# A layer stack on one core: a shorter load of x ahead of the key weights, two fewer dummy matmuls, and the order lists that go with it

## The chip, the cores and the metric

The kernel runs on one core of a Trainium2 chip. The metric is the device time of one execution in microseconds (us); lower is better. Three runs of the kernel before gave 327.53, 329.68 and 484.78 us, with a median of 329.68. The profiled execution took 327.5 us.

## The reference

Two layers, each applied twice with the same weights: a linear attention (32 heads of 16) and an MLP with gelu. The input of each is normalised first, and the MLP normalises it a second time inside. All inputs and the output are bf16; x is 2048 x 512.

```python
def _A_ref(x, wqkv, wo):                    # D = 512, H = 32, Dh = 16
    q, k, v = split(x @ wqkv)
    phi = lambda t: jnp.where(t > 0, t + 1, jnp.exp(t)) + 1e-6
    pq, pk = phi(q), phi(k)
    kv = jnp.einsum("bhsd,bhse->bhde", pk, v)
    z = jnp.einsum("bhsd->bhd", pk)
    num = jnp.einsum("bhqd,bhde->bhqe", pq, kv)
    den = jnp.einsum("bhqd,bhd->bhq", pq, z)[..., None] + 1e-6
    return (num / den).reshape(B, S, D) @ wo

def _B_ref(x, w1, b1, w2, b2):              # F = 1792
    h = _gelu(_layernorm(x) @ w1 + b1)
    return h @ w2 + b2

x = x + _A_ref(_layernorm(x), wqkv, wo)
x = x + _B_ref(_layernorm(x), w1, b1, w2, b2)
x = x + _A_ref(_layernorm(x), wqkv, wo)
x = x + _B_ref(_layernorm(x), w1, b1, w2, b2)
```

## The kernel before

**Tiles.** The 2048 tokens are 16 tiles of 128, in 4 chunks of 4. Tile `st` is tile `k` of chunk `c` (`st = 4c + k`). In the names of operations the first digit is the round (0 or 1), the rest the tile or chunk: `K0_5` is the key projection of tile 5 in the first round.

**What is done to a tile of x in the first round.** VectorE takes its statistics (`statsA0_`, line 773, and `aggrA0_`, line 775); VectorE or GpSimd adds epsilon (`vepsA0_`, line 780); GpSimd raises it to the power -1/2 (`powA0_`, line 782); VectorE or ScalarE normalises it (`normA0_`, lines 795 and 790). Tile 3 takes its sums on ScalarE (`sumA0_3` and `sqA0_3`, lines 764 and 768, with `negA0_3` on GpSimd between). The tile is then transposed: tiles 0 to 5 on TensorE (`PTA0_`, line 817) with a copy out of PSUM (`tcA0_`, line 827), the others by a transposing DMA that SP issues (`TA0_`, line 804). Four matmuls make the keys (`K0_`, line 866), ScalarE and VectorE apply phi (`expk0_`, `reluk0_`, `mink0_`, `phik0_`, lines 837 to 854), and four matmuls add the tile to the Gram matrix of normalised x and phi of the keys (`G0_`, line 958). `Z0_` (line 941) sums the keys over the tokens, `Q0_` (lines 883 and 896) makes the queries. The key sums and the matrix go through small operations (`zb`, `KV`, `M`, `cp`) to one 512-wide matrix, `WO` applies it, and `D` (line 1074) or a sum on VectorE makes the denominators.

**The MLP** is `W1` (line 1127), gelu on ScalarE (line 1132) and `W2` (line 1163); in the last round the result goes out through the stores `OD` that SP issues.

**Dummies.** TensorE begins with matmuls of constant ones into a PSUM bank that nothing reads (`warm0`, `warm1`, line 747). `WARM` holds their widths, one list per operation.

**Loads.** `LOADS` gives each load a name, its queue (SP or ScalarE), what it loads (x by chunk and tiles, or the halves of the key or query weights), the range, and a load or operation behind which it is issued. Tile 0 of x is `x0`, tiles 1 to 3 are `x1`, `wk0` and `wk1` are the halves of the key weights, `xc1` to `xc3` the other chunks of x, `wq` the query weights. The rest of the weights go out on GpSimd's queue once all transposes of the first round are there (`wv`, `wo`, `w1_`, `w2_`). `b2` (128 KB, one row spread to 128 partitions) and `b1` go out on SP's queue; `b1` overwrites a zeroed buffer (`b1z`, GpSimd), and `Tb1` transposes it.

**Order.** Nothing is scheduled on the chip: `ORDER` lists, for each of the five engines, every operation in the order of issue, `PLACES` lists which tile uses which buffer slot after which, and `WAY` picks an engine or a form for some operations. `Settled` reads them, `assign_waits` puts a semaphore wait in front of an operation only where an earlier wait does not imply it. An engine runs its list strictly in order, so an operation that waits holds everything behind it; SP's transposes, stores and loads are one such list.

Of the kernel before, what the change touches and what calls it, by code (L numbers as in the profile page):

```python
# [185 lines left out]
def assign_waits(graph, order, sems, dma_sems):  # L186
# [10 lines left out]
    while len(done) < total:  # L197
        moved = False
        for e in ENGINES:
# [42 lines left out]
    WARM=[[512, 512, 512, 512, 512, 512, 512, 512, 512, 512, 512], [512, 512, 512, 512]],  # L242
    LOADS=[['x0', 'sp', 'x', 0, 0, 1, ''], ['x1', 'sp', 'x', 0, 1, 4, ''], ['wk0', 'sp', 'wk', 0, 0, 2, ''], ['wk1', 'act', 'wk', 0, 2, 4, 'ones'], ['xc1', 'act', 'x', 1, 0, 4, 'x0'], ['xc3', 'act', 'x', 3, 0, 4, ''], ['wq', 'act', 'wq', 0, 0, 4, ''], ['xc2', 'act', 'x', 2, 0, 4, '']],
    ORDER={
        "sp":
            "x0 x1 wk0 TA0_7 TA0_6 TA0_8 TA0_14 TA0_15 TA0_13 TA0_12 b2 TA0_10 TA0_11 TA0_9 b1 Tb1 TB0_1 TB0_0 TB0_2 TB0_3 "
            "TP0_2_0 TP0_2_1 TB0_7 TB0_4 TB0_5 TB0_6 TP0_2_3 TP0_3_3 TP0_2_2 TP0_3_2 TA1_0 TB0_9 TB0_10 TB0_8 TP0_3_1 TP0_3_0 "
            "TB0_11 TA1_5 TB0_15 TB0_12 TB0_14 TB0_13 TA1_2 TA1_7 TA1_3 TA1_1 TA1_6 TA1_4 TA1_9 TA1_8 TA1_10 TA1_11 TA1_12 "
            "TA1_13 TA1_15 TA1_14 TP1_1_0 TP1_1_1 TP1_1_2 TB1_2 TB1_3 TP1_1_3 TP1_3_1 TB1_5 TB1_4 TB1_7 TB1_6 OD1 TP1_3_0 "
            "TP1_2_1 TP1_3_3 OD0 TP1_2_0 TP1_3_2 TP1_2_3 TP1_2_2 OD2 TB1_15 TB1_13 TB1_12 TB1_14 OD5 OD3 TB1_10 TB1_9 TB1_11 "  # L250
            "TB1_8 OD7 OD4 OD13 OD6 OD14 OD12 OD10 OD8 OD9 OD11 OD15_0 OD15_1",
        "pe":
            "warm0 warm1 PTA0_0 PTA0_1 K0_0 PTA0_2 K0_1 PTA0_3 K0_2 PTA0_4 G0_0_0 K0_3 K0_4 Q0_0_0 G0_1_0 PTA0_5 Q0_0_1 K0_5 "
            "G0_2_0 Z0_0 G0_3_0 K0_6 K0_7 K0_8 G0_4_0 Q0_1_2 K0_14 G0_5_0 K0_15 G0_6_0 G0_7_0 Q0_1_0 K0_12 Z0_1 K0_13 K0_10 "
            "K0_11 K0_9 Q0_1_3 Q0_1_1 Q0_0_3 Q0_0_2 G0_8_0 Z0_3 Z0_2 G0_9_0 G0_10_0 D0_0_0 G0_11_0 G0_12_0 D0_0_2 G0_13_0 "
            "G0_14_0 D0_0_3 D0_0_1 D0_1_1 G0_15_3 D0_1_0 G0_15_1 G0_15_2 ZR0 G0_15_0 Q0_2_0 Q0_2_1 KV0_0 KV0_1 KV0_2 KV0_3 "
            "Q0_2_2 M0_1 M0_0 M0_3 D0_1_2 M0_2 Q0_2_3 WO0_0_0 D0_1_3 WO0_0_1 WO0_0_2 WO0_0_3 WO0_1_0 WO0_3_0 WO0_2_0 Q0_3_1 "
            "Q0_3_0 WO0_4_0 WO0_7_0 WO0_5_0 Q0_3_2 Q0_3_3 WO0_6_0 W10_0_0_0 W10_0_13_0 W10_0_3_0 W10_0_2_0 W10_0_6_0 "
            "W10_0_9_0 W10_0_11_0 W10_0_5_0 W10_0_8_0 W10_0_1_0 W10_0_4_0 W10_0_12_0 W10_0_10_0 W10_0_7_0 W20_0_0 W20_1_0 "
            "W10_0_2_1 W10_0_7_1 W10_0_5_1 W10_0_11_1 W20_0_7 W20_1_7 W10_0_1_1 W10_0_9_1 W10_0_12_1 WO0_9_0 W10_0_0_1 "  # L260
            "W10_0_6_1 W10_0_8_1 W10_1_1_0 W10_1_6_0 WO0_8_0 W10_0_4_1 W10_1_7_0 W10_1_10_0 W10_1_8_0 W10_1_11_0 W10_1_3_0 "
            "W10_1_9_0 W10_0_13_1 W10_1_5_0 W10_1_4_0 W10_1_13_0 WO0_11_0 W10_1_0_0 W10_1_12_0 W10_1_2_0 W10_0_3_1 W10_0_10_1 "
            "WO0_15_0 W20_4_0 W20_5_0 W20_5_7 WO0_10_0 W20_4_7 K1_0 WO0_14_0 W20_7_0 W20_6_0 W20_7_7 W20_6_7 W20_3_0 W20_2_0 "
            "W20_2_7 WO0_13_0 W10_2_6_0 W10_2_0_0 WO0_12_0 W10_2_5_0 W20_3_7 W10_2_12_0 W10_2_9_0 W10_2_4_0 W10_2_3_0 "
            "W10_2_2_0 W10_2_1_0 W10_2_13_0 W10_2_8_0 W10_2_11_0 W10_2_10_0 W10_2_7_0 W20_10_0 W20_11_0 W20_9_0 W20_9_7 "
# [12 lines left out]
            "W21_6_0 W21_5_0 W21_4_0 W21_5_7 W21_4_7 W11_3_10_0 W11_3_0_0 W21_7_0 W11_3_7_0 W11_3_1_0 W21_6_7 W11_3_3_0 "
            "W11_3_2_0 W21_7_7 W11_3_8_0 W11_2_7_0 W11_3_11_0 W11_3_13_0 W11_3_4_0 W11_3_6_0 W11_3_12_0 W11_2_9_0 W11_3_9_0 "
            "W11_3_5_0 W11_2_3_0 W11_2_5_0 W21_14_0 W11_2_2_0 W21_13_0 W21_12_0 W11_2_6_0 W21_12_7 W21_13_7 W11_2_11_0 "  # L280
            "W11_2_0_0 W21_14_7 W11_2_4_0 W11_2_13_0 W11_2_1_0 W11_2_12_0 W11_2_8_0 W11_2_10_0 W21_8_0 W21_9_0 W21_10_0 "
            "W21_8_7 W21_10_7 W21_9_7 W21_15_h0 W21_11_0 W21_11_7 W21_15_h1",
        "act":
            "wk1 xc1 xc3 sumA0_3 wq sqA0_3 tcA0_0 xc2 tcA0_1 expk0_0 tcA0_2 reluk0_0 tcA0_3 expk0_1 reluk0_2 reluk0_1 tcA0_4 "
            "expk0_2 reluk0_3 expk0_3 normA0_7 expq0_0_0 expk0_4 tcA0_5 reluq0_0_0 normA0_8 expk0_5 reluq0_0_1 normA0_14 "
            "expq0_0_1 reluk0_5 expk0_6 normA0_15 expk0_8 normA0_13 reluk0_8 expk0_7 expk0_14 reluk0_7 normA0_10 expq0_1_2 "
            "reluk0_14 expk0_15 normA0_11 expq0_1_0 expk0_12 reluk0_13 expk0_13 expk0_10 reluk0_11 expk0_11 expk0_9 "
            "reluq0_1_3 expq0_1_3 reluq0_1_1 expq0_0_3 expq0_1_1 expq0_0_2 reluq0_0_2 ln0_0_0 rec0_0_0 ln0_0_2 rec0_0_2 "
            "ln0_0_3 ln0_0_1 rec0_0_3 cpz0 rec0_0_1 expq0_2_0 ln0_1_1 rec0_1_1 ln0_1_0 rec0_1_0 cpm0_0 cpm0_1 expq0_2_1 "
# [1040 lines left out]
```

## Time and profile before

The page of the profiled execution, 327.5 us by the clock of the runs, with a span of 326.3 us from the first to the last instruction:

| | busy us | share of the span | instructions |
|---|---|---|---|
| TensorE matmul (PE) | 322.2 | 99% | 1723 |
| TensorE weight load (PEld) | 159.3 | 49% | 1723 |
| VectorE (DVE) | 211.0 | 65% | 503 |
| ScalarE (ACT) | 193.1 | 59% | 334 |
| GpSimd (POOL) | 152.5 | 47% | 224 |

Busy time counts an engine's instructions whatever they wait for next; a matmul's own length (0.63 us at the start, 0.38 us later, for 512 columns) holds its way through the array, so the time between two starts is the better measure of what one costs. The chain of waits goes back from the last instruction, at each step to what released it. "Idle before, releaser" behind a row is how long the engine had stood and what ended that. SPq, ACTq and POOLq are the queues of these engines, with their DMA issues.

Loads move 20.4 MB in all. In the first 12 us they are 3.15 MB.

### The profile page before, as it was taken

Reading aid. Unit: us, or ns where it says so; the run is one execution under the profiler, and the core shown is the slowest. Engines: PE = TensorE matmul, PEld = TensorE weight load, DVE = VectorE, ACT = ScalarE, POOL = GpSimd, SP = SyncE. Lnnn points to the kernel's source line nnn. Section 1 sums busy time; section 2 is a strip of 40 time slices with the busy share of each in tenths; the row PEclk is TensorE's granted clock in tenths of the full one; section 3 lists DMA queues with packets and bytes.
Section 4 is the critical chain, followed back from the end, with each engine's and each line's share of the span. In section 5 each row is a group of like instructions: output and inputs, shape, how many; then the busy total and the mean of one; then the engine's idle time right before and its main releaser. Section 6 shows DMA issues by size and latency. Waiting matters only on the chain.

```text
span 326.3 us, 4763 instructions
## 1 busy us (share of the span) xinstructions
PE 322.2 (99%) x1723; PEld 159.3 (49%) x1723; DVE 211.0 (65%) x503; ACT 193.1 (59%) x334; POOL 152.5 (47%) x224
## 2 busy tenths in 40 slices
PE   8999999999999999999999999999999999999997
PEld 3444445576454444444444444458644444444444
DVE  5987679996938685142436899999989983300112
ACT  4988769797661416529673477969833454551600
POOL 5662548588663417300757434783856593100000
PEclk9999999999999999999999999999999999999999
DMA  7355753334012210331011110012034322200102
GB/s 266 120 83 97 219 189 104 105 64 68 16 32 50 54 26 3 80 64 34 0 32 33 34 32 0 19 32 50 17 82 94 69 48 66 64 0 2 64 0 80
DMA packets 46883, 20.37 MB, mean 62 GB/s; under 512 B 41932, under 2 KB 45388, under 8 KB 46860
## 3 DMA queue, kind: packets, MB, share of 16 engines
q1 hardware_dynamic: 44572, 13.00, 18.8%
q0 software_dynamic: 1056, 4.72, 4.5%
q10 hardware_dynamic: 1232, 2.36, 2.0%
q8 instruction: 13, 0.21, 0.3%
q14 instruction: 10, 0.08, 0.1%
HBM read 8.00 MB, written 2.10 MB: 31 GB/s over the span
## 4 chain that ended last, share of the span: by engine, by line
PE 97%; DVE 1%; ACT 1%; issue 0%
PE ps L1127 30%; PE ps L1163 29%; PE ps L1097 9%; PE ps L866 8%; PE ps L883 5%; PE ps L987 4%; PE ps L958 4%; PE ps L896 2%; PE ps L747 2%; PE ps L1150 1%; PE ps L1074 1%; PE ps L1008 1%; PE ps L1031 1%; PE ps L941 1%; PE ps L817 0%; DVE pkb L854 0%
## 5 line engine op out<-in xcount | busy, mean ns | idle before, releaser
L1132 ACT ACTIVATE gT<-ps,b1c 128x512 bf16<-128x512 f32 (+1 forms) x140 | 77.1, 600 | 65.3 <-PE ps L1127 65.0
L1127 PE MATMUL ps<-t,w 128*128 128x512 bf16 (+1 forms) x560 | 102.2, 336 | 0.0
L1163 PE MATMUL ps<-w,gT 128*128 128x512 bf16 x434 | 97.6, 379 | 0.0
L1127 PEld LDWEIGHTS ps<-t,w 128*128 128x128 bf16 x560 | 54.6, 98 | 43.7 <-ACT t L827 0.3
L1163 PEld LDWEIGHTS ps<-w,gT 128*128 128x128 bf16 x434 | 42.5, 98 | 50.4 <-DVE xsb L1169 0.2
L782 POOL TENSOR_TENSOR rstd<-veps,neghalf 128x1 f32<-128x1 f32 x64 | 37.9, 602 | 33.5 <-DVE veps L780 31.4
L837 ACT ACTIVATE eb<-ps 128x512 bf16<-128x512 f32 x64 | 37.4, 614 | 18.3 <-PE ps L866 10.5
L1173 DVE TENSOR_TENSOR outb<-ps,xsb 128x512 bf16<-128x512 f32 x15 | 10.1, 686 | 46.3 <-PE ps L1163 40.3
L773 DVE BATCH_NORM_STATS2 stats<-xsb 128x6 f32<-128x512 f32 x48 | 32.3, 678 | 0.4
L848 ACT ACTIVATE rb<-ps 128x512 bf16<-128x512 f32 x45 | 26.6, 617 | 9.2 <-PE ps L866 8.7
L866 PE MATMUL ps<-wqkv,t 128*128 128x512 bf16 x128 | 31.6, 379 | 0.1
L1097 PE MATMUL ps<-gtb,t 128*128 128x512 bf16 x128 | 31.2, 379 | 0.1
L850 DVE TENSOR_SCALAR eb<-eb 128x512 bf16<-128x512 bf16 x45 | 14.0, 321 | 21.1 <-ACT eb L837 21.1
L1113 POOL TENSOR_TENSOR xsb<-xsb,b2b 128x512 f32<-128x512 f32 x20 | 24.3, 1224 | 6.8 <-ACT yb L790 6.6
L790 ACT ACTIVATE yb<-xsb,nmr,rstd 128x512 bf16<-128x512 f32 x21 | 16.7, 812 | 14.2 <-POOL nmr L787 13.9
L780 POOL TENSOR_SCALAR veps<-mv 128x1 f32<-128x1 f32 x35 | 7.6, 217 | 30.8 <-DVE mv L775 28.1
L1063 POOL TENSOR_TENSOR t<-t,rr 128x512 bf16<-128x512 bf16 x14 | 15.5, 1114 | 13.6 <-DVE rr L1059 12.9
L795 DVE TENSOR_SCALAR yb<-xsb,mv,rstd 128x512 bf16<-128x512 f32 x27 | 16.1, 602 | 8.5 <-POOL rstd L782 8.3
L1051 POOL TENSOR_TENSOR lr<-t,zrow 128x512 f32<-128x512 bf16 x15 | 17.9, 1191 | 5.7 <-ACT zrow L971 4.2
L883 PE MATMUL ps<-wqkv,t 128*128 128x512 bf16 x80 | 19.9, 379 | 0.0
L1097 PEld LDWEIGHTS ps<-gtb,t 128*128 128x128 bf16 x128 | 12.3, 98 | 14.7 <-DVE rr L1059 0.6
L866 PEld LDWEIGHTS ps<-wqkv,t 128*128 128x128 bf16 x128 | 12.0, 98 | 14.9 <-ACT t L827 1.0
(97 smaller groups left out, 373.5 us busy)
## 6 DMA issues: line engine op xcount, KB each, us to landing
w<-in_B_w_dram POOLq DMA_DIRECT2D x4, 896.0 KB, 6.9
out_dram<-outb SPq DMA_DIRECT2D x15, 128.0 KB, 1.9
t<-in_A_x_dram ACTq DMA_DIRECT2D x3, 512.0 KB, 4.6
t<-yb SPq DMA_TRANSPOSE x56, 2.5
wqkv<-in_A_wqkv_dram ACTq DMA_DIRECT2D x1, 512.0 KB, 5.8
wqkv<-in_A_wqkv_dram POOLq DMA_DIRECT2D x1, 512.0 KB, 4.6
wo<-in_A_wo_dram POOLq DMA_DIRECT2D x1, 512.0 KB, 5.5
t<-in_A_x_dram SPq DMA_DIRECT2D x1, 384.0 KB, 3.1
```

The lines of the kernel that those rows point to most:

```text
L773: G.op("dve", lambda e: e.bn_stats(stats[:, s.slot, :], src()), 620, reads=src_keys, writes=[k + "s"], tiles=[s, *src_tiles], name=f"stats ...
L782: G.op("pool", lambda e: e.tensor_tensor(rstd[:, s.slot:s.slot + 1], veps[:, s.slot:s.slot + 1], neghalf[:], op=ALU.pow), 570, reads=[k + ...
L837: G.op("act", lambda e: e.activation(eb[:, et.slot, :], bank(bt), ACT.Exp), 478, reads=[src_key], writes=[f"e{tag}"], tiles=[bt, et], name ...
L848: G.op("act", lambda e: e.activation(rb[:, rt.slot, :], bank(bt), ACT.Relu), 478, reads=[src_key], writes=[f"r{tag}"], tiles=[bt, rt], nam ...
L866: ins = e.matmul(bank(b), lhsT=yTa(yT)[:, dt, k * P:(k + 1) * P], rhs=wqkv[:, dt, D:2 * D], start=(dt == 0), stop=(dt == DT - 1))
L883: ins = e.matmul(bank(b), lhsT=yTa(yT)[:, dt, k * P:(k + 1) * P], rhs=wqkv[:, dt, 0:D], start=(dt == 0), stop=(dt == DT - 1))
L1051: lambda e, r=r, tok=tok: e.tensor_tensor(lr[:, r.slot, :], tok(), zrow[:], op=ALU.mult), 1150 if on_pool else 600,
L1097: ins = e.matmul(bank(wb), lhsT=yTa(pq)[:, kt, k * P:(k + 1) * P], rhs=gtb[:, kt, :], start=(kt == 0), stop=(kt == DT - 1))
L1113: G.op("pool" if on_pool else "dve", lambda e: e.tensor_tensor(xsb[:, st, :], xsb[:, st, :], b2b[:], op=ALU.add), 1120 if on_pool else 600 ...
L1127: ins = e.matmul(bank(b, n), lhsT=w1[:, dt, ft * P:(ft + 1) * P], rhs=yTa(yT)[:, dt, k0 * P:k1 * P], start=(dt == 0), stop=(dt == DT - 1))
L1132: G.op("act", lambda e, ft=ft, b=b, k0=k0, k1=k1, n=n: e.activation(gT[:, g.slot, ft * 512 + k0 * P:ft * 512 + k1 * P], bank(b, n), ACT.Ge ...
L1163: ins = e.matmul(bank(b), lhsT=gT[:, g.slot, ft * 512 + k * P:ft * 512 + (k + 1) * P], rhs=w2[:, ft, :], start=(ft == 0), stop=(ft == FT - 1))
```

## The change

`LOADS` splits the load of tiles 1 to 3 of x: tile 1 alone stays in front (`x1`), tiles 2 and 3 (`x2`) go out on ScalarE's queue behind the second half of the key weights. `WARM` has 13 dummies instead of 15, and the first transpose on TensorE stands between the first 11 and the last 2. The five order lists, 56 of 68 lists of buffer slots and 61 entries of `WAY` are written anew with it; no operation but `x2` is added and none but the two dummies is removed.

```diff
-    WARM=[[512, 512, 512, 512, 512, 512, 512, 512, 512, 512, 512], [512, 512, 512, 512]],
-    LOADS=[['x0', 'sp', 'x', 0, 0, 1, ''], ['x1', 'sp', 'x', 0, 1, 4, ''], ['wk0', 'sp', 'wk', 0, 0, 2, ''], ['wk1', 'act', 'wk', 0, 2, 4, 'ones'], ['xc1', 'act', 'x', 1, 0, 4, 'x0'], ['xc3', 'act', 'x', 3, 0, 4, ''], ['wq', 'act', 'wq', 0, 0, 4, ''], ['xc2', 'act', 'x', 2, 0, 4, '']],
+    WARM=[[512, 512, 512, 512, 512, 512, 512, 512, 512, 512, 512], [512, 512]],
+    LOADS=[['x0', 'sp', 'x', 0, 0, 1, ''], ['x1', 'sp', 'x', 0, 1, 2, ''], ['wk1', 'act', 'wk', 0, 2, 4, 'ones'], ['wk0', 'sp', 'wk', 0, 0, 2, ''], ['x2', 'act', 'x', 0, 2, 4, ''], ['xc1', 'act', 'x', 1, 0, 4, 'x0'], ['xc3', 'act', 'x', 3, 0, 4, ''], ['wq', 'act', 'wq', 0, 0, 4, ''], ['xc2', 'act', 'x', 2, 0, 4, '']],
     ORDER={
         "sp":
-            "x0 x1 wk0 TA0_7 TA0_6 TA0_8 TA0_14 TA0_15 TA0_13 TA0_12 b2 TA0_10 TA0_11 TA0_9 b1 Tb1 TB0_1 TB0_0 TB0_2 TB0_3 "
...
+            "x0 x1 wk0 TA0_7 TA0_6 TA0_8 b2 TA0_14 TA0_15 TA0_13 TA0_12 TA0_10 TA0_11 TA0_9 b1 Tb1 TB0_1 TB0_0 TP0_2_0 TB0_2 "
...
         "pe":
-            "warm0 warm1 PTA0_0 PTA0_1 K0_0 PTA0_2 K0_1 PTA0_3 K0_2 PTA0_4 G0_0_0 K0_3 K0_4 Q0_0_0 G0_1_0 PTA0_5 Q0_0_1 K0_5 "
-            "G0_2_0 Z0_0 G0_3_0 K0_6 K0_7 K0_8 G0_4_0 Q0_1_2 K0_14 G0_5_0 K0_15 G0_6_0 G0_7_0 Q0_1_0 K0_12 Z0_1 K0_13 K0_10 "
-            "K0_11 K0_9 Q0_1_3 Q0_1_1 Q0_0_3 Q0_0_2 G0_8_0 Z0_3 Z0_2 G0_9_0 G0_10_0 D0_0_0 G0_11_0 G0_12_0 D0_0_2 G0_13_0 "
...
+            "warm0 PTA0_0 warm1 PTA0_1 K0_0 PTA0_2 K0_1 K0_2 PTA0_4 PTA0_3 G0_0_0 K0_3 Q0_0_1 K0_4 Q0_0_0 PTA0_5 G0_1_0 "
+            "G0_2_0 G0_3_0 K0_5 K0_7 K0_6 Z0_0 K0_8 Q0_1_2 K0_14 G0_4_0 G0_5_0 G0_6_0 K0_15 Q0_1_0 G0_7_0 K0_12 K0_13 Z0_1 "
+            "K0_10 K0_11 K0_9 Q0_1_3 Q0_1_1 Q0_0_3 G0_8_0 Q0_0_2 Z0_3 Z0_2 G0_9_0 G0_10_0 D0_0_0 G0_11_0 D0_0_2 D0_0_3 "
...
         "act":
-            "wk1 xc1 xc3 sumA0_3 wq sqA0_3 tcA0_0 xc2 tcA0_1 expk0_0 tcA0_2 reluk0_0 tcA0_3 expk0_1 reluk0_2 reluk0_1 tcA0_4 "
...
+            "wk1 x2 xc1 xc3 wq tcA0_0 sumA0_3 tcA0_1 sqA0_3 expk0_0 tcA0_2 reluk0_0 xc2 expk0_1 tcA0_3 tcA0_4 expk0_2 "
...
         "dve":
-            "ones statsA0_0 aggrA0_0 vepsA0_0 normA0_0 statsA0_1 aggrA0_1 vepsA0_1 statsA0_2 aggrA0_2 normA0_1 statsA0_4 "
-            "aggrA0_4 normA0_2 statsA0_5 normA0_3 statsA0_7 mink0_0 normA0_4 phik0_0 aggrA0_5 statsA0_12 aggrA0_7 mink0_1 "
...
+            "ones statsA0_0 aggrA0_0 statsA0_1 aggrA0_1 normA0_0 normA0_1 statsA0_2 aggrA0_2 vepsA0_2 statsA0_4 normA0_2 "
+            "aggrA0_4 statsA0_6 statsA0_7 mink0_0 normA0_4 normA0_3 phik0_0 statsA0_5 mink0_1 aggrA0_6 aggrA0_5 aggrA0_7 "
...
         "pool":
-            "id0 eps6 bdm0 bdm1 neghalf id1 powA0_0 negA0_3 b1z powA0_1 vepsA0_2 powA0_2 vepsA0_3 powA0_3 vepsA0_4 powA0_4 "
...
-            "nmrA0_11 wv wo w1_0 w1_1 phik0_14 phiq0_1_1 w2_0 pr0_0_3 pr0_0_1 pr0_1_1 pz0_2_0 w2_1 pr0_1_2 pr0_1_3 powB0_1 "
...
+            "id0 bdm0 neghalf id1 vepsA0_0 powA0_0 vepsA0_1 powA0_1 negA0_3 powA0_2 vepsA0_3 vepsA0_4 powA0_4 powA0_3 "
...
```

The new GpSimd list has, from the weights on, `wv wo phik0_14 w1_0 w1_1 bdm1 phiq0_1_1 b1z w2_0 w2_1`; `eps6` comes later too.

## The prediction, made before the changed kernel ran

> **What bounds the kernel now.** I read the chain of waits first, then TensorE's own waits, then the first 14 us instruction by instruction, then the DMA issues behind which something waits. By engine and by line, the chain is
>
> ```profile
> PE 97%; DVE 1%; ACT 1%; issue 0%
> ```
>
> so the end is set by one unbroken row of matmuls, and TensorE's waits are almost nothing:
>
> ```profile
> PE ps L747 <- PEq L1315: 0.8, 1, 0.8
> PE ps L941 <- DVE pkb L854: 0.7, 1, 0.7
> PE ps L817 <- DVE yb L795: 0.2, 1, 0.2
> ```
>
> The second row is `Z0_2` at 39.84 us, the third `PTA0_1`. A full-clock 512-column matmul starts 0.216 us after the last one (28 in 6.04 us in the chain). Counting each matmul at such a spacing, all real ones need 315 us; what lies between the first dummy (0.84) and the last matmul (324.1) beyond that is 6.2 us of dummies and 2.0 us of waits. Outside it are 0.84 us ahead, 2.1 us of output behind (324.1 to 326.3), and 1.2 us outside the span (327.5 - 326.3).
>
> The first turn, in start, length, engine (start of the span on the left):
>
> ```profile
> 0.84 6.34 PE L747 MATMUL ps<-const-bfloat16-1.0 128*128 128x512 bf16 x15 [0.84 <-PEq L1315]
> 3.21 0.69 DVE L773 BATCH_NORM_STATS2 stats<-t 128x6 f32<-128x512 bf16 x1 [1.75 <-DMA t<-in_A_x_dram]
> 4.39 0.56 POOL L782 TENSOR_TENSOR rstd<-veps,neghalf 128x1 f32<-128x1 f32 x1 [0.80 <-DVE veps L780]
> 4.99 0.41 DVE L795 TENSOR_SCALAR yb<-t,mv,rstd 128x512 bf16<-128x512 bf16 x1 [0.68 <-POOL rstd L782]
> 5.49 0.15 PEld L747 LDWEIGHTS ps<-const-bfloat16-1.0 128*128 128x128 bf16 x1 [0.28 <-issue]
> 5.91 0.15 PEld L747 LDWEIGHTS ps<-const-bfloat16-1.0 128*128 128x128 bf16 x1 [0.28 <-issue]
> 7.01 0.39 PE L817 MATMUL ps<-idp,yb 128*128 128x128 bf16 x4
> 7.43 0.60 ACT L827 ACTIVATE t<-ps 128x512 bf16<-128x512 bf16 x1 [1.09 <-PE ps L817]
> 8.09 1.04 PE L866 MATMUL ps<-wqkv,t 128*128 128x512 bf16 x4
> 8.34 0.38 DVE L795 TENSOR_SCALAR yb<-t,mv,rstd 128x512 bf16<-128x512 bf16 x1
> 8.96 0.39 PE L817 MATMUL ps<-idp,yb 128*128 128x128 bf16 x4
> ```
>
> The reader is to see that the first tile is normalised at 5.40 and yet transposed only at 7.01, behind the dummies. These start every 0.427 us (5.49, 5.91), twice the later spacing, although the granted clock of this stretch reads 1.00; the last one, at 6.76, gave way after 0.25 us, so the faster spacing came at about 6.8.
>
> **The change, part by part.** *Dummies.* 15 become 11, then `PTA0_0`, then 2. Two fewer at 0.427 us are 0.85 us, the most the opening can gain.
>
> *First turn.* The 11 end at 0.84 + 11 x 0.427 = 5.54. VectorE now does tile 2's statistics before it normalises tile 1, and GpSimd takes tile 1's veps (row of 0.25 us, next start 0.33 later, for 0.15 on VectorE): aggregate done 4.12, power done 4.15 + 0.33 + 0.56 = 5.05, tile 1 normalised 5.1 to 5.5, 0.1 later than now. `PTA0_0` at 5.6; slow, a quarter of a dummy each, 0.43 us. Two dummies to 6.9. ScalarE copies 6.25 to 6.85. Tile 2 (aggregate 4.95, power 5.4 to 5.95 behind tile 1's) is normalised by 6.4, `PTA0_1` goes at 6.9, `K0_0` at 7.1 for 8.09 now.
>
> *Loads.* x1 shrinks from 384 to 128 KB and x2 (256 KB) goes out on ScalarE's queue behind wk1. The landings in the trace are x0 3.19, x1 4.40, wk1 5.47, wk0 6.21: 1 MB by 6.21. The same 1 MB stands in front of tiles 3 and 4 now, so I put x2 at 5.5 to 6.2 (4.40 at the lowest), before VectorE asks for it at 6.4. The weights are needed at 7.1, not later than now. Free, with 0.2 us of cover for x2. On ScalarE's queue xc1, xc3 and wq move one issue (0.43 us) back, and xc2 behind five operations.
>
> *Second turn.* Tile 3: statistics 6.35 to 7.0, aggregate and veps to 7.25, power 7.35 to 7.95, behind statsA0_4 on VectorE, normalised 8.0 to 8.4 (8.34 to 8.72 now). TensorE has finished `K0_0` at 7.97 and stands until 8.45: a new wait of 0.5 us, with K0_1 queued behind it in order, which starts at 8.7 (9.18 now). ScalarE's sumA0_3 and sqA0_3 come behind tcA0_0 and tcA0_1, so tcA0_2 ends at 9.7 and `K0_2` starts at 9.75 (10.30 now). `G0_0_0` needs phik0_0, and VectorE now has aggrA0_4, two statistics (0.62 each), mink0_0, normA0_4 and normA0_3 in front of it: done 11.1, `G0_0_0` at 11.2 for 11.40. So VectorE eats most of the 0.85: **-0.2 us** (between -0.2 and -0.5) is left.
>
> *b2 moved forward on SP's queue*, from behind TA0_12 to behind TA0_8. What it does to the transpose behind it stands in the trace (issues in narrow windows; last number us to landing):
>
> ```profile
> b2b<-in_B_b_dram SPq DMA_DIRECT2D x1, 128.0 KB, 3.9
> ```
>
> ```profile
> t<-yb SPq DMA_TRANSPOSE x1, 4.1
> ```
>
> b2 was issued at 26.80 and landed at 30.73; TA0_10, issued 27.43, landed at 31.49, 0.76 behind b2 and after 4.1 us, where its neighbours took 2.4 to 2.6. `K0_10` started 0.14 us after it. Now TA0_14 is the one behind: TA0_8 goes out at about 18.1 and takes 1.27, b2 0.58, TA0_14 at 20.0, b2 lands at 19.4 + 3.9 = 23.3, TA0_14 at 24.1. Its user `K0_14` has also moved one G group (four matmuls, 0.86) forward: 24.24 - 0.86 - 0.2 = 23.2. TensorE stands from 23.2 to 24.25 (24.1 + 0.14): 1.1 us. Lower bound 0 (landing after 2.5 us, at 22.5), upper 1.3; TA0_14 itself took 3.6 us now, with no load ahead of it, which would be 23.6 and 0.6 us of wait; I take 1.1, since TA0_10 is the same instruction behind the same load. In exchange K0_10's 0.08 us go.
>
> *Moved with no cost.* b1 now waits for b1z on GpSimd, behind phiq0_1_1 (about 40 us); SP has nothing between 34.6 and 58.98, and b1c is needed at 61. bdm1 (0.84) moves behind the issue of w1_1 and ends near 38.6, ahead of zb0 at 41; without that cover it would cost the difference directly. 61 small operations trade engine (VectorE 503 to 506, GpSimd 220 to 217); both have room (65% and 47%).
>
> *All other order lists and buffer places.* The matmuls are the same. Walking the new TensorE list at the present spacings and setting each group against when its inputs were ready, I find no group more than a few us ahead of its producer that is not preceded by the same shift of that producer. The nearest rows for a new wait are the present ones: 0.8 us at `Z0_2`, 0.3 at `WO1_15_0`. I take 0, with -1.0 (both go) to +1.5 (two more like the longest).
>
> **Sum.** -0.2 + 1.1 = +0.9 us on 327.5: **328.4 us**. The median of the runs is 329.68, of 327.53, 329.68 and 484.78; the profiled time is at the bottom of these. About 2% (6.6 us) is what a measurement of this kernel can tell from no change.
>
> **The rivals.** *1, the opening gain arrives (0.22).* SP's queue does not hold TA0_14, as 2.5 us of most transposes say; against it is TA0_10. Then -0.2 to -0.85 and at best Z0_2's 0.8: 325.9 to 327.3. Faster by 2% it cannot become: even without every wait and with the first real matmul at 5.6, 5.6 + 315 + 2.1 + 1.2 = 323.9.
>
> *2, slower: the faster matmul spacing comes later (0.20).* Dummies began at 0.84 and the change came at about 6.8, after 6.0 us of unbroken work. Now `PTA0_0` and a short idle stand at 5.5 to 6.0, just before that point. If the 6.0 us have to be run anew from there, the change comes at 12.0: work from 6.9 to 12.0 at half rate, half of 5.1 us lost, less the 0.5 us for which TensorE would wait for VectorE anyway: +2.0, in all 330.4. It decides when the matmuls of `K0_0` are 0.427 us apart. For it: the place of the break; against: it is short, and the first dummies began out of a pause too.
> The Trainium skill, "TensorE: Matmul & The Clock Gate" (Part 1: The HAM clock gate), says that the array starts at half clock and goes to full after a busy window of about 3.4 us that runs free of the kernel, and (Part 4: PE-mode transpose) that transposes do not count as busy in the same way, which speaks against a transpose among the dummies. The trace agrees on half rate (0.427 against 0.216 us) and shows only the one switch; by that rule, an estimate, one lost window would cost at most 1.7 us, less the 0.5: 329.6.
>
> *3, slower: the new order breaks somewhere (0.08).* For 6.6 us, several late landings must each hold TensorE, as TA0_14 does, or one must miss by the 4.1 us of a held transpose and a second follow. Against: the same kind of list left 2.0 us of waits now. It would give 334 to 337. It decides if one wait over 4 us appears.
>
> *4, the first turn is not earlier at all (part of the 0.50).* If x2 lands 0.5 us later than 6.2, tile 3 sets the pace and the head stays at 0: 328.6.
>
> **How the numbers follow.** Forecast with case 4: 0.50, 327.3 to 329.3; rival 1 0.22, rival 2 0.20, rival 3 0.08. The likeliest is 328.4. The range leaves out rival 3 and the lowest part of rival 1: from 326.4 to 331.5, the top being rival 2's 330.4 and 1.1 of the 1.5 us of unknown waits, which also takes in a run like that of 329.68. Faster by over 2%: 0.02; within 2%: 0.90; slower: 0.08.
>
> **What the new profile would show.** Right: PE L747 x13, `K0_0` near 7.1, a wait of about 0.5 us before the third transpose, a TensorE wait near 23 on the transpose behind b2, TA0_14 landing after about 4 us, the rest unbroken. Wrong: no wait at 23 (rival 1), 0.427 us spacing in the first K groups (rival 2), a wait over 4 us anywhere (rival 3).

## The result, and the profile after

The kernel after took 332.44 us (median of four runs, 331.26 to 334.09) beside 329.11 for the kernel before: a ratio of 1.0114, with a 95% interval of 1.0078 to 1.0149. The 329.11 is the median of four runs of which one, of 484.78 us, is a slow one that the ratio leaves out. A second sample on another chip (the first of the experiments below) gave 1.0070 (1.0038 to 1.0102). Within 2%, then, but slower by 0.7 to 1.1%, and outside the predicted range of 326.4 to 331.5 us. The profiled execution took 331.26 us with a span of 329.1, 2.8 more than the 326.3 of before; the other 0.9 us between the two profiled times (331.26 and 327.5) lie outside the spans, where 2.2 us stand for 1.2 before, and the trace doesn't show what they are. The spans of the other three runs are 330.7 to 332.8 us, so this profile too is at the bottom of its runs. Line numbers are three lower after the change (L747 is now L744, L817 L814, L866 L863, L773 L770, L795 L792, L941 L938, L1127 L1124). The prediction and the expectations count tiles from one: their tile 3 is `statsA0_2` and `normA0_2`. The text here goes by the numbers in the names, from 0.

The chain that ended last, by engine, on the page of the kernel after:

```profile
PE 86%; DMA 6%; DVE 3%; ACT 2%; issue 1%; POOL 1%; SPq 0%; ACTq 0%
```

Before it was 97% PE. Now the chain leaves the row of matmuls for DMAs and VectorE. TensorE's own waits say where (engine, line, who was waited for: us in total, times, longest):

```profile
PE ps L863 <- DMA t<-yb: 1.7, 1, 1.7
PE ps L814 <- DVE yb L792: 1.7, 1, 1.7
PE ps L744 <- PEq L1312: 0.8, 1, 0.8
PE ps L1124 <- DMA t<-yb: 0.8, 1, 0.8
PE ps L938 <- DVE pkb L851: 0.2, 1, 0.2
```

Without the third row, which is the start and the same in both, these are 4.4 us, where before had 0.9. That is 3.5 us more waiting, less two dummies of 0.427 us: +2.65 of the 2.8 us. The account closes on these waits, with the 0.2 us at `PTA0_1` that are gone: the third transpose (`PTA0_2`, L814, +1.7), `K0_14` (L863, +1.7), a new one in the last MLP (`W11_3_10_0`, L1124, +0.8), and `Z0_2` (L938), whose 0.7 shrank to 0.2.

The opening, from the timeline of the kernel after (start, length, engine, line; idle time before and what ended it in brackets):

```profile
0.84 4.85 PE L744 MATMUL ps<-const-bfloat16-1.0 128*128 128x512 bf16 x11 [0.84 <-PEq L1312]
...
5.59 0.61 PE L814 MATMUL ps<-idp,yb 128*128 128x128 bf16 x4
...
6.67 0.69 DVE L770 BATCH_NORM_STATS2 stats<-t 128x6 f32<-128x512 bf16 x1 [0.21 <-DMA t<-in_A_x_dram]
...
6.88 1.04 PE L863 MATMUL ps<-wqkv,t 128*128 128x512 bf16 x4
...
8.52 0.69 DVE L770 BATCH_NORM_STATS2 stats<-t 128x6 f32<-128x512 bf16 x1 [0.76 <-DMA t<-in_A_x_dram]
9.13 0.40 DVE L792 TENSOR_SCALAR yb<-t,mv,rstd 128x512 bf16<-128x512 bf16 x1
...
9.59 0.40 PE L814 MATMUL ps<-idp,yb 128*128 128x128 bf16 x4 [1.67 <-DVE yb L792]
```

The first half went as hoped: `PTA0_0` at 5.59, `K0_0` at 6.88 for 8.09 before, its four matmuls, 1.04 us long together, already at the faster spacing. Then VectorE stands idle for 0.76 us, until 8.52. The statistics operation that it starts there is `statsA0_4`, of tile 4, which comes with `xc1`; `normA0_2`, whose input had been ready at 8.41 (the power of tile 2 ran from 7.85 for 0.56), is queued behind it. The load `xc1` landed at 7.49 before and at 8.50 now, though it was issued at the same time (3.21 and 3.24). In the kernel before, `statsA0_4` started without a wait:

```profile
7.51 0.69 DVE L773 BATCH_NORM_STATS2 stats<-t 128x6 f32<-128x512 bf16 x1
```

The two later waits, in the timeline of TensorE, with the row of `K0_14` before in front:

```profile
24.24 1.03 PE L866 MATMUL ps<-wqkv,t 128*128 128x512 bf16 x4
...
26.02 1.02 PE L863 MATMUL ps<-wqkv,t 128*128 128x512 bf16 x4 [1.73 <-DMA t<-yb]
...
273.94 1.90 PE L1124 MATMUL ps<-t,w 128*128 128x512 bf16 x7 [0.78 <-DMA t<-yb]
```

And what they waited for, in narrow windows of the DMA view (last number: us from issue to landing; the row of q8 is the queue of instruction fetches in the window 23 to 25 us: transfers, MB, share):

```profile
b2b<-in_B_b_dram SPq DMA_DIRECT2D x1, 128.0 KB, 3.3
...
t<-yb SPq DMA_TRANSPOSE x1, 4.8
...
q8 instruction: 1, 0.02, 2.9%
...
out_dram<-outb SPq DMA_DIRECT2D x1, 128.0 KB, 2.2
...
t<-yb SPq DMA_TRANSPOSE x1, 4.0
```

The first pair is `b2` (landed 23.77) and `TA0_14` behind it (25.88); the second is the store `OD2` (271.51) and `TB1_13` behind it. In both, a 16 KB instruction fetch also lies inside the transpose: at 23.86 to 24.81 and from 271.73.

### The profile page after: what moved, and what is told of

Same layout as the page of the kernel before. It is cut to its first block, busy times and chain, and to the rows that moved or that the text cites. A ratio compares the mean times of both kernels' runs of the same rounds, so it can differ in the third digit from the quotient of the medians.

```text
span 329.1 us, 4720 instructions
## 1 busy us (share of the span) xinstructions
PE 320.0 (97%) x1691; PEld 158.9 (48%) x1721; DVE 215.7 (66%) x506; ACT 191.5 (58%) x334; POOL 147.5 (45%) x221
## 4 chain that ended last, share of the span: by engine, by line
PE 86%; DMA 6%; DVE 3%; ACT 2%; issue 1%; POOL 1%; SPq 0%; ACTq 0%
PE ps L1124 29%; PE ps L1160 26%; PE ps L1094 8%; PE ps L863 6%; PE ps L880 5%; PE ps L984 4%; DMA t<-yb 3%; PE ps L955 3%; DMA t<-in_A_x_dram 2%; PE ps L893 1%; DVE stats L770 1%; ACT gT L1129 1%; PE ps L1147 1%; PE ps L1071 1%; PE ps L1005 1%
## 5 line engine op out<-in xcount | busy, mean ns | idle before, releaser
L1129 ACT ACTIVATE gT<-ps,b1c 128x512 bf16<-128x512 f32 (+1 forms) x140 | 76.2, 602 | 63.6 <-PE ps L1124 63.3
L1124 PE MATMUL ps<-t,w 128*128 128x512 bf16 (+1 forms) x553 | 101.7, 336 | 1.2 <-DMA t<-yb 0.8
L1124 PEld LDWEIGHTS ps<-t,w 128*128 128x128 bf16 x560 | 54.5, 98 | 44.7 <-DMA t<-yb 1.3
L777 POOL TENSOR_SCALAR veps<-mv 128x1 f32<-128x1 f32 x38 | 9.5, 249 | 54.1 <-DVE mv L772 51.5
L863 PE MATMUL ps<-wqkv,t 128*128 128x512 bf16 x125 | 30.9, 379 | 2.0 <-DMA t<-yb 1.7
L770 DVE BATCH_NORM_STATS2 stats<-xsb 128x6 f32<-128x512 f32 x48 | 32.2, 677 | 0.2
L1110 POOL TENSOR_TENSOR xsb<-xsb,b2b 128x512 f32<-128x512 f32 x21 | 25.1, 1204 | 4.1 <-DVE yb L792 2.9
L1060 POOL TENSOR_TENSOR t<-t,rr 128x512 bf16<-128x512 bf16 x15 | 17.4, 1165 | 10.7 <-DVE rr L1056 7.9
L847 DVE TENSOR_SCALAR eb<-eb 128x512 bf16<-128x512 bf16 x45 | 13.3, 300 | 13.5 <-ACT eb L834 13.3
L1166 DVE TENSOR_TENSOR xsb<-ps,xsb 128x512 f32<-128x512 f32 x16 | 10.9, 684 | 16.0 <-PE ps L1160 16.0
L863 PEld LDWEIGHTS ps<-wqkv,t 128*128 128x128 bf16 x128 | 11.9, 97 | 16.7 <-DVE veps L777 2.2
L880 PE MATMUL ps<-wqkv,t 128*128 128x512 bf16 x78 | 19.6, 379 | 0.1
L1048 POOL TENSOR_TENSOR lr<-t,zrow 128x512 f32<-128x512 bf16 x12 | 14.8, 1230 | 7.0 <-ACT zrow L968 4.0
```

Source lines behind the costliest of these rows:

```text
L770: G.op("dve", lambda e: e.bn_stats(stats[:, s.slot, :], src()), 620, reads=src_keys, writes=[k + "s"], tiles=[s, *src_tiles], name=f"stats ...
L863: ins = e.matmul(bank(b), lhsT=yTa(yT)[:, dt, k * P:(k + 1) * P], rhs=wqkv[:, dt, D:2 * D], start=(dt == 0), stop=(dt == DT - 1))
L880: ins = e.matmul(bank(b), lhsT=yTa(yT)[:, dt, k * P:(k + 1) * P], rhs=wqkv[:, dt, 0:D], start=(dt == 0), stop=(dt == DT - 1))
L1060: lambda e, d=d, tok=tok, heads=heads: e.tensor_tensor(heads(tok()), heads(tok()), rr[:, d.slot, :].unsqueeze(2).broadcast_to([P, H, DH]), ...
L1110: G.op("pool" if on_pool else "dve", lambda e: e.tensor_tensor(xsb[:, st, :], xsb[:, st, :], b2b[:], op=ALU.add), 1120 if on_pool else 600 ...
L1124: ins = e.matmul(bank(b, n), lhsT=w1[:, dt, ft * P:(ft + 1) * P], rhs=yTa(yT)[:, dt, k0 * P:k1 * P], start=(dt == 0), stop=(dt == DT - 1))
```

## The experiments

The theory after the result: two parts cost, the split load (through `xc1` and what stands behind it on VectorE) and `b2` in front of `TA0_14`; fewer dummies gain next to nothing; the rest of the rewritten lists costs nothing. The rivals: the rewritten lists as a whole are worse; the dummies matter, through the spacing or by their own time; the base was only a lucky execution. Sixteen kernels ran, each ratio against runs of the kernel before on the same chip (25 to 35 of them, with medians of 328.88 to 329.63).

**The kernel after again, unaltered.**

> The changed kernel once more, unaltered, beside the next three. Theory (a fixed wait at the third transpose, and one at K0_14 whose length depends on where an instruction fetch of 16 KB falls): the third transpose again starts at 9.4 to 9.7 us; TA0_14 again lands behind b2, and takes over 4 us if the fetch falls between its issue and its landing, otherwise 3.0 to 3.4; the time is 1.5 to 3.0 us over the kernel before. Rival (the switch to the fast matmul spacing decides): executions with a later switch are the longer ones, by half of the delay.

331.17 us, ratio 1.0070 (1.0038 to 1.0102). The same waits, the first one longer: `xc1` lands at 8.99, `PTA0_2` starts at 10.08 after 2.36 us, `TA0_14` takes 4.9 us with a fetch at 24.39 inside, `K0_14` starts at 26.53 after 1.82 us, and `W11_3_10_0` waits 1.0 us.

**The first suspected wait taken out of after**

```diff
-statsA0_4 normA0_2
+normA0_2 statsA0_4
```

> The changed kernel with one exchange on VectorE: normA0_2 in front of statsA0_4. Theory (three separate waits, each behind a load): the third transpose no longer waits for the landing of xc1 and starts at about 8.9 instead of 9.59 us, so the wait before it falls from 1.67 to about 1.0 us; but K0_14 is tied to the landing of TA0_14 (25.9 us), so the gain is lost there and the time stays within 0.4 us of the changed kernel, 3 us over the kernel before. Rival (the opening alone sets the pace): the time falls by the 0.7 us of the earlier transpose.

1.0034 (1.0006 to 1.0063). The wait at `PTA0_2` shrinks from 1.67 to 1.03 us, not to nothing: tile 2 itself comes with `x2`, which lands near 6.7. In this execution no fetch met `TA0_14`: it took 3.2 us behind `b2`, and `K0_14` hardly waited, so the gain is not that of the swap alone.

**b2 back behind TA0_12 in after**

```diff
-TA0_8 b2 TA0_14 TA0_15 TA0_13 TA0_12 TA0_10
+TA0_8 TA0_14 TA0_15 TA0_13 TA0_12 b2 TA0_10
```

> The changed kernel with b2 back behind TA0_12 on SP's queue, nothing else. Theory (TA0_14 cannot start before b2 has landed): TA0_14 lands after 2.5 to 3.6 us, at or before 24.0 us, K0_14 waits 0.3 us or less instead of 1.9, and the time falls by 1.5 to 2.2 us, to 1.2 to 1.8 us over the kernel before. Rival (TA0_14 is late because its normalisation is 0.9 us later and an instruction fetch falls on it): TA0_14 still takes over 4 us and the time falls by 0.5 us at most.

1.0053 (1.0036 to 1.0070, four runs of the kernel). `TA0_14` takes 2.42 us and `K0_14` starts at 24.20 without a wait; `TA0_10` behind `b2` takes 3.6 in its place, and TensorE stands 0.75 us in front of `K0_10`.

**The loads of before in after**

```diff
-LOADS=[['x0', 'sp', 'x', 0, 0, 1, ''], ['x1', 'sp', 'x', 0, 1, 2, ''], ['wk1', 'act', 'wk', 0, 2, 4, 'ones'], ['wk0', 'sp', 'wk', 0, 0, 2, ''], ['x2', 'act', 'x', 0, 2, 4, ''],
+LOADS=[['x0', 'sp', 'x', 0, 0, 1, ''], ['x1', 'sp', 'x', 0, 1, 4, ''], ['wk0', 'sp', 'wk', 0, 0, 2, ''], ['wk1', 'act', 'wk', 0, 2, 4, 'ones'],
...
-"wk1 x2 xc1 xc3
+"wk1 xc1 xc3
```

> The changed kernel with the loads of the kernel before: x1 is tiles 1 to 3 again on SP's queue, x2 is gone. Theory: xc1 lands at about 7.5 instead of 8.50 us, statsA0_4 and the third transpose come 0.9 to 1.0 us earlier (8.6), and the gain is lost at K0_14, so the time is within 0.4 us of the changed kernel. Rival (the split of the load does no harm, the dummies or the order of VectorE do): the third transpose still starts after 9.2 us.

1.0011 (0.9981 to 1.0042), by the ratio the largest step of the three, though the intervals overlap. The time was expected to stay within 0.4 us of the kernel after, and that is a miss. `xc1` lands at 8.00, `PTA0_2` starts at 9.10 after 0.95 us. The profiled execution (330.33 us, over the median of 329.79) still has the `K0_14` wait of 1.6 us (`TA0_14` 4.65 us behind `b2`, with a fetch).

**The swap, b2 back, and OD2 behind TB1_13, in after**

```diff
-TB1_14 OD2 TB1_13
+TB1_14 TB1_13 OD2
```

> The changed kernel with three exchanges: normA0_2 in front of statsA0_4, b2 back behind TA0_12, OD2 behind TB1_13. Theory: the three waits account for all of the loss; none over 1.0 us is left at the third transpose, none over 0.3 at K0_14 and at W11_3_10_0, and the time is 2.5 to 3.5 us under the changed kernel, within 0.7 us of the kernel before. Rival (the switch to the fast matmul spacing comes later in some executions, or the rewritten lists lose time in many places): over 1.5 us of the loss stays.

1.0017 (1.0000 to 1.0035). The wait at `K0_14` is gone (`TA0_14` 2.42 us) and that at `W11_3_10_0` is down to 0.2 us (`TB1_13` 2.5 us). The third transpose, with the load still split, waits 1.31 us (`PTA0_2` 9.04), where 1.0 at most was expected.

**The split load alone, in before** (the diff of the loads above, the other way round)

> The kernel before with the split load alone (x1 is tile 2, x2 on ScalarE's queue ahead of xc1). Theory: xc1 lands at 8.3 to 8.5 us instead of 7.5, statsA0_4 waits for it, the third transpose starts at about 9.6 instead of 8.8 us, and the time rises by 0.6 to 1.0 us. Rival (the first load of another chunk is hidden): the third transpose stays within 0.2 us of 8.8 and the time does not change.

1.0033 (1.0008 to 1.0058): +0.9 us. The timeline of TensorE in it, at `PTA0_1`:

```profile
8.76 0.40 PE L817 MATMUL ps<-idp,yb 128*128 128x128 bf16 x4 [2.54 <-DVE yb L795]
```

With the order of before it is another queue that pays: `sumA0_3` on ScalarE waits for `x2` (landed 6.50), `negA0_3` on GpSimd for that (7.33), `powA0_1` is queued behind it (7.69 for 6.49 before), and `normA0_1` ends at 8.71. Again nothing of tile 1 needs `x2`; it stands behind something that does.

**b2 forward alone, in before** (the diff of `b2` above, the other way round)

> The kernel before with b2 moved behind TA0_8 alone. Theory: b2 goes out at 19.8 and lands at 23.0 to 24.5 us, TA0_14 lands 0.5 to 2.1 us behind it instead of at 23.5, K0_14 (24.2) waits 0.3 to 1.8 us, and the time rises by 0.2 to 1.5 us, less the 0.08 us that K0_10 no longer waits. Rival (the transpose does not wait for the load): TA0_14 lands before b2, and the time is unchanged within 0.2 us.

1.0030 (1.0004 to 1.0055): +1.1 us, and in the timeline of TensorE the predicted wait in its predicted place:

```profile
25.22 1.02 PE L866 MATMUL ps<-wqkv,t 128*128 128x512 bf16 x4 [1.10 <-DMA t<-yb]
```

The two parts alone (0.9 and 1.1) make up 2.0 of the 2.3 us that the kernel after was above before in the same comparison (331.17 and 328.88). By the intervals each part alone is worth between 0.1 and 1.9 us, so the match of the sum is better than the measurements warrant.

**Both undone in after, the rest of its lists kept** (the diffs of the loads and of `b2` together)

> The kernel after with the two parts undone that cost something alone in the kernel before (the loads as before, without x2; b2 behind TA0_12 again), and all its other order lists and buffer places kept. If these two are the whole loss: equal to before, ratio 1.000, within 0.4 us. If the rest of the rewritten lists costs something that these two hide (the wait of 0.8 us before W11_3_10_0 behind OD2, for one): 0.6 to 1.0 us above before. If the fewer dummies give their 0.85 us once nothing takes their place: 0.5 to 0.9 us below.

328.45 us beside 328.89, 0.9983 (0.9961 to 1.0004): equal to before or a little below. Nothing else in the rewritten lists costs what can be measured, and the gain of the fewer dummies does not show either. The wait before `W11_3_10_0` is in this profile, with 0.9 us, but the profiled execution (329.46 us) was the slowest of the eleven.

**Two more moves on top of it** (the swap of `normA0_2`, and `OD2` behind `TB1_13`)

> The kernel after with the two parts undone (loads as before, b2 behind TA0_12), and OD2 behind TB1_13, normA0_2 ahead of statsA0_4 as well. The kernel with the two alone undone lay 0.4 us below before, with a wait of 0.9 us at W11_3_10_0 left in its trace. If that wait is a loss of most executions: 0.7 to 1.3 us below before. If it falls only where a fetch meets TB1_13: 0.2 to 0.6 us below, as without OD2's move.

A miss: 1.0029 (1.0010 to 1.0048), slower than without them. Its `W11_3_10_0` wait is gone, but with the loads of before the swap does harm: `xc1` is there early (`statsA0_4` starts at 7.62 without the swap), `normA0_2` cannot run before 8.4 either way, and `statsA0_4` now starts at 8.76. `PTA0_4` is 0.6 us later (11.41 for 10.81) and TensorE waits four times for VectorE, 2.2 us in all. So, as far as one trace tells (its execution, 328.28 us, was the fastest of the twelve), the order that mends the split load is wrong for the whole one.

**Fewer dummies alone, in before**: 13, a second time 13, and 11 in place of 15

```diff
-512, 512, 512], [512, 512, 512, 512]]
+512, 512, 512], [512, 512]]
```

> The kernel before with 13 dummies in front of the first transpose in place of 15, nothing else. Dummies eaten by VectorE (my theory): the third transpose still waits for normA0_2, which ended at 8.72 in the trace of before and does not depend on the dummies, so at most 0.1 us is gained from there on: within 0.4 us of before, either way. Dummies are worth their time: two of 0.427 us, 0.85 us less. Dummies are what brings the faster spacing: it comes later than 6.8 and the first K groups run at 0.427 us a matmul, 1 to 2 us more.

> The kernel before with 13 dummies, a second sample of it on another chip. Its trace showed nothing gained (K0_0 0.31 us earlier, K0_14 0.29 later), its lowest time equals that of before (327.24 and 327.39), but its median lay 1.2 us below. If the dummies are eaten by VectorE and the medians only fell differently: ratio within 0.2% of 1.000, lowest times equal within 0.3 us. If the dummies are worth their 0.85 us: 0.7 to 1.3 us below again, in the lowest time too.

> The kernel before with 11 dummies in place of 15 (nine and two). Eaten by VectorE: the third transpose still at 8.7 to 8.9, within 0.4 us of before. Worth their time: the four would bring up to 1.7 us, and at least the two further ones 0.85 over the kernel with 13. The faster spacing later: K0_0 at 0.427 us a matmul, 1 to 2 us above before.

With 13, 0.9972 (0.9951 to 0.9993), then 0.9995 (0.9969 to 1.0021), which includes no change. The medians, though, were 1.2 and 1.1 us below before (327.67 beside 328.89, 327.88 beside 329.00), while the lowest times of before and of these are 327.24 to 327.49, all four. The times alone therefore leave open whether 13 gains a little. With 11, 1.0021 (1.0002 to 1.0039). The timeline of TensorE shows what becomes of the time at the start: `PTA0_1` of the kernel with 13,

```profile
7.59 0.40 PE L817 MATMUL ps<-idp,yb 128*128 128x128 bf16 x4 [0.77 <-DVE yb L795]
```

and `PTA0_1` and `PTA0_2` of the kernel with 11:

```profile
7.58 0.40 PE L817 MATMUL ps<-idp,yb 128*128 128x128 bf16 x4 [1.72 <-DVE yb L795]
...
9.18 0.40 PE L817 MATMUL ps<-idp,yb 128*128 128x128 bf16 x4 [0.34 <-DVE yb L795]
```

Whatever is taken from the dummies comes back as a wait for `normA0_1`, and `PTA0_1` starts at 7.58 or 7.59 (7.63 in the second sample with 13, 7.58 in the prediction's profile with 15). In these traces VectorE eats the dummies; why the two medians with 13 lay lower isn't shown.

**The kernel before again**

> The kernel before, unaltered, as a second sample: ratio 1.000 within 0.3 us, which is what the comparisons can tell apart. Its profile is a second look: if the base was a lucky one, this look has a span over 326.9 us, with a wait of TensorE at K0_14 or another place where a transpose met an instruction fetch; if before has no such waits, the span is 326.3 within 0.3 us.

1.0001 (0.9977 to 1.0024). Its profiled execution has a span of 327.7 us, 1.4 above the execution that the prediction was made on. TensorE's waits in it that matter:

```profile
PE ps L817 <- DVE yb L795: 0.9, 1, 0.9
...
PE ps L941 <- DVE pkb L854: 0.7, 1, 0.7
PE ps L1097 <- DMA t<-t: 0.7, 2, 0.4
```

The first is not a loss (the faster spacing came earlier here, and VectorE ate that too); the third is new. And `K0_14`, at 24.24 in the first execution, starts at 24.63, 0.14 us after `TA0_14` landed, which took 4.11 us with a fetch inside it (3.60 in the first). Nothing had been moved in front of that transpose. This is the lead for the next table. Laid side by side matmul by matmul, the second execution is 0.2 us ahead at `K0_0`, 0.39 behind at `K0_14`, 0.69 at 81 us (line 1127) and 1.44 behind the two waits at L1097. The two transposes that these wait for, at 246 and 249 us, met no fetch and took 2.5 and 2.4 us. But a fetch at 242.97 lies inside `TB1_7`, four places ahead on SP's list (4.28 us for 2.60), the issue of `TB1_6` behind it took 2.06 us for 1.27, and SP's list went on that much later. So a fetch can also cost a transpose that it does not touch, through the order of the queue.

**The fetch.** All 18 profiled executions have `TA0_14`, and they differ in two things: whether `b2` stands in front, and whether a 16 KB fetch lies inside it.

| `b2` in front | fetch inside | executions | issue to landing, us |
|---|---|---|---|
| no | no | 3 | 2.40 to 2.42 |
| no | yes | 10 | 3.60 to 4.61 |
| yes | no | 1 | 3.18 |
| yes | yes | 4 | 4.65 to 4.96 |

In the ten with a fetch alone it began 0.9 to 2.0 us after the issue, in the four with `b2` as well 2.2 to 3.0 us after it, so each time before the transpose would have landed without it (2.4 and 3.18 us); in the four without a fetch inside, it began after the landing. So the transposes are not merely longer and for that reason likelier to contain one. The same program with and without the fetch, in the DMA view: the kernel with 13 dummies, first sample (the queue's row is for 20 to 24 us),

```profile
t<-yb SPq DMA_TRANSPOSE x1, 4.3
...
q8 instruction: 1, 0.02, 1.9%
```

and its second sample, which has no row of that queue between 20 and 22.4 us:

```profile
t<-yb SPq DMA_TRANSPOSE x1, 2.4
```

The same holds for the 1008 transposes of normalised tiles in these executions: 2.41 to 2.56 us (10th to 90th percentile, median 2.49) for the 777 with neither; median 3.5 with a fetch inside for over 0.3 us (111 of them). For those with a plain transfer still under way on SP's queue the median stays 2.5 without a fetch (70), and is 4.1 with one (24). Taken by where the fetch begins, with no plain transfer ahead: all 74 transposes in whose first 2.1 us a fetch began took 2.65 us or more (median 3.9), and of the 775 in which none began from 1.2 us before the issue to the landing, 26 took over 2.7.

Nor is the fetch thrown at random. Counted in TensorE's weight loads, the first comes at number 94 to 123 in the 18 executions, the second at 246 to 255, the twelfth at 1453 to 1460: much the same place of TensorE's program each time, within 30, 10 and 8 weight loads. That these fetches are TensorE's is inferred from this count. The first place is just in front of `K0_14`, while `TA0_14` is under way; the twelfth is where `OD2` and `TB1_13` had been moved to. The Trainium skill, "Runtime: NRT & Kernel Launch" (Instruction fetch mechanics), says that an engine's instructions are refilled in 16 KiB blocks of 256 instructions by a DMA queue of the sequencer's own, at a cost that is mostly hidden. The trace agrees on the size, and on a distance that is most often 110 to 140 weight loads, each with its matmul; TensorE shows no wait of its own for it. What it does not hide is the 1.2 to 2.2 us by which a transposing DMA under way is later.

**The waits of before covered with other work**, in before

```diff
-Q0_1_2 K0_14 G0_5_0 K0_15 G0_6_0 G0_7_0
+Q0_1_2 G0_5_0 K0_14 G0_6_0 K0_15 G0_7_0
...
-phik0_6 zs0_0 mink0_8 phiq0_0_1 phik0_5 mink0_7
+phik0_5 phik0_6 zs0_0 mink0_8 phiq0_0_1 mink0_7
...
-Z0_3 Z0_2 G0_9_0 G0_10_0 D0_0_0 G0_11_0
+Z0_3 G0_9_0 Z0_2 G0_10_0 G0_11_0 D0_0_0
```

and `b2` behind `Tb1`.

> The kernel before with other work put in front of its two places where TensorE waits or comes close to it: G0_5_0 in front of K0_14 and G0_6_0 in front of K0_15 (phik0_5 in front of phik0_6 on VectorE for it), so that a transpose lengthened by an instruction fetch is covered for 0.86 us more; b2 behind Tb1; G0_9_0 in front of Z0_2, which waited 0.66 us, and G0_11_0 in front of D0_0_0. If these waits are what the executions lose: 0.66 us and, where a fetch falls on TA0_14, up to 0.9 us more, so 0.7 to 1.5 us below before. If each wait is only passed on to the next operation: within 0.4 us of before.

1.0001 (0.9976 to 1.0025), a miss. `TA0_14` took 4.18 us and `K0_14` did not wait, `Z0_2` did not either; but the profile has 0.7 us at two other DMA landings (L1097, again behind a `TB1_7` of 4.1 us with a fetch inside), and no median gain.

**The same for Z0_2 and b2 alone, with 13 dummies**

> The kernel before with 13 dummies, b2 behind Tb1, and G0_9_0 put in front of Z0_2 with G0_11_0 in front of D0_0_0, whose wait of 0.66 us went in the trace of the earlier kernel with that change. If a wait in the middle is won to the end: 0.4 to 0.7 us below the kernel with 13 dummies alone, in the lowest time too. If it is passed on: equal to it within 0.3 us.

0.9989 (0.9967 to 1.0011), with the lowest time of all (326.95 us) and 1.1 us of waits at L1097. Inconclusive: the 0.9 us of it stand behind a transpose of 2.4 us without a fetch, issued 1.0 to 1.4 us later than in the executions with 13 and 15 dummies (249.37 for 248.39 and 248.01); a fetch had met `OD1` and `TP1_3_0` ahead of it on SP's list (3.7 and 3.6 us). That what is won at one wait is lost to the fetches further on is a reading of these traces, not shown by a run.

**A version rearranged for both** (after with the loads of before, tile 2 before tile 4 on VectorE, ScalarE's sums of tile 3 first, `b2` behind `Tb1`, `OD2` behind `TB1_13`)

```diff
-normA0_0 normA0_1 statsA0_2 aggrA0_2 vepsA0_2 statsA0_4 normA0_2
+normA0_0 statsA0_2 normA0_1 aggrA0_2 vepsA0_2 normA0_2 statsA0_4
```

> The changed kernel with the loads of the kernel before, tile 3 taken before tile 5 on VectorE, the sums of tile 4 before the first copy on ScalarE, b2 behind Tb1 where nothing waits, and OD2 behind TB1_13. Theory (the 13 dummies are worth what the first turn can use, once no load stands in the way): the third transpose follows K0_0 without a wait at about 8.0 us, none at K0_14 and W11_3_10_0, and the time is 0.3 to 1.0 us under the kernel before. Rival (the second turn is bound by VectorE whatever the loads do): the lead is gone by G0_0_0 (11.3 us) and the time equals the kernel before within 0.3 us.

0.9992 (0.9968 to 1.0016): before again. Here `x1` landed at 5.27 and `normA0_0`, behind `statsA0_1` which waits for it, let `PTA0_0` start only at 6.56; `TA0_14` took 4.6 us with no plain transfer ahead of it, only a fetch, and `K0_14` waited 1.2 us. No version was shown in two samples to beat the kernel before.

## Why the prediction was wrong

**The base.** The sum of +0.9 was put on 327.5 us, and the prediction itself said that this was at the bottom of the runs. It is: 120 further runs of before have medians of 328.88 to 329.63 us, and 327.4 to 327.6 at the lowest. Of the 4.0 us between 328.4 and 332.44, 1.6 are the base (329.11 - 327.5). Either error alone would have left the time inside the range: 329.11 + 0.9 is 330.0, and 327.5 with the measured 3.3 us is 330.8. The second execution of before shows one thing that an execution at the bottom lacks: a fetch in front of something that is needed soon, 0.75 of the 1.4 us at L1097. The prediction's 2% for what can be told from no change was too wide as well: the intervals of these comparisons are 0.2 to 0.4% either way.

**The head, -0.2, was +0.6.** Right: 0.85 from the dummies, `K0_0` near 7.1 (6.88), the new wait in front of the third transpose, and its form, `normA0_2` behind `statsA0_4` on VectorE. Wrong: its size, 0.5 against 1.67 us (the wait of 0.2 at `PTA0_1` went in exchange). The failing step is "Free" under *Loads*, with xc1's place in the queue priced at nothing. The 256 KB were set against the weights and tile 2; they also stand in front of `xc1`. Its issue did not move by the 0.43 us of the prediction, but it landed 1.0 us later (7.49 to 8.50), and `statsA0_4` kept its old place in the sum, done before a normalisation at 8.0. The kernel with the swap and the split load alone in before show both halves. With the loads of before the wait is still 0.84 to 0.95 us, so 0.3 to 0.5 of the 1.17 us by which it was under-priced lie in the sum for VectorE, and the other 0.7 to 0.8 in the split load.

**K0_14, +1.1, was +1.7.** The mechanism, the place and the engine were right, and the part alone measured +1.1 us. The term was mis-sized since `TA0_14` was priced like `TA0_10`, at 0.8 us behind `b2`; it landed 2.1 behind. Besides, `b2` landed 0.5 us later than planned (23.77 for 23.3), and TensorE came to `K0_14` 1.1 us later (24.29 for 23.2), which hid as much. The 3.6 us that `TA0_14` had taken "with no load ahead of it" were in the prediction, without what goes with them in the traces: the fetch, which comes on top of `b2` (3.18 us behind `b2` without one, 4.65 to 4.96 with one).

**All other lists, 0 with -1.0 to +1.5.** In the profile: 0.8 at `W11_3_10_0` and 0.5 off `Z0_2` (0.66 us in the trace of before, 0.8 in the prediction), so +0.3; in the medians of the kernel with both parts undone, nothing. Right.

**The rivals.** 1 fell: SP's queue did hold `TA0_14`, and the opening gain did not arrive. 2 did not happen: the faster spacing had come before `K0_0`. By the spacing of the dummies it came between about 3.6 and 6.8 us in the 18 executions. In the three in which `PTA0_0` clearly stood in front of it among the dummies (the kernel after, the one with the swap and the one with both parts undone) it came at 6.1 to 6.4, so the transposes did not visibly put it off. So the Trainium skill's point that PE-mode transposes do not count as busy in the same way ("TensorE: Matmul & The Clock Gate", Part 4) cost nothing here. 3 had no wait over 4 us. 4 came closest: the head is not earlier, `x2` was 0.4 us later than 6.2 (landed 6.64, `statsA0_2` starts on it at 6.67), and tile 2 alone would have cost 1.0 us of wait, as the swap showed.

## What to carry to other kernels

When a load is put ahead in a queue, follow every load behind it to its first user, and then everything that is queued in order behind that user, on its engine and on the engines that wait for that: both times a tile that did not need the load paid. Time taken from a filler can come back as a wait while the engine that feeds the next step sets the pace, as here at `PTA0_1`; look for that wait. And before a sum is put on one profiled execution, see where that stands among the runs: here a second profile moved the base by 1.4 us, more than the whole predicted effect.

## What the runs showed of the hardware

A transposing DMA of a 128x512 tile takes 2.4 to 2.6 us in most cases here. `TA0_14` took 3.6 to 4.6 us in all ten executions in which a 16 KB instruction fetch began while it was under way, and 2.40 to 2.42 in the three without; behind a plain 128 KB load it took 3.18 without and up to 4.96 with a fetch. The fetches come at much the same places of TensorE's program in every execution, and a transpose that is held up also makes those behind it on SP's list late. This rests on what the traces show side by side, and on the same program with and without the fetch. Not tried: moving the place of the fetch itself by adding or removing TensorE instructions far ahead of it, and why a transposing DMA is held up by up to 2.2 us when the fetch itself lasts 0.9 to 1.6.
